# First expert rounds: most weight tiles planned behind the token gather, and all coarse flags on VectorE

## The chip, the cores and the metric

The kernel runs on one core of a Trainium2 chip. The metric is the device time in microseconds (us) of one execution; less is better. The engines are named as the profile does: PE is TensorE's matmuls and PEld its weight loads, DVE is VectorE, ACT is ScalarE, POOL is GpSimd, and SP is SyncE, which issues transfers.

## What is computed

```python
# attention: batch 8, heads 8, seq 576, head_dim 64; heads 0-3 a window of 32, heads 4-7 a dilated window (4 * 32)
scores = scale * np.matmul(q, k.transpose(0, 1, 3, 2))
scores = np.where(masks[None, :, :, :], scores, -1000000000.0)
attn = np.exp(scores - np.max(scores, axis=-1, keepdims=True))
attn = attn / (np.sum(attn, axis=-1, keepdims=True) + 1e-09)
x = np.matmul(attn, v)                    # -> (4608, 512)
# mixture of experts: N, D, E, F = 4608, 512, 8, 1024; cap = N // E
for idx in np.argsort(-(x @ w_gate).flatten()):
    tok, e = (int(idx) // E, int(idx) % E)
    if assigned[tok] >= 0 or counts[e] >= cap:
        continue
    assigned[tok] = e
    counts[e] += 1
for e in range(E):
    mask = assigned == e
    h = np.maximum(x[mask] @ w1[e], 0.0)
    out[mask] = h @ w2[e]
```

All tokens are ranked against all experts, and every expert takes exactly 576 tokens, each with its own best free choice in the order of the gate's values. Then each expert runs two matrix products on its tokens.

## The kernel before

The attention goes over 8 batches. Each makes scores (L485, L502, L505), exponentials (L455), the product with `v` (L513), the transposes of its result (L563) and the gate's logits (L596, L655). The result `xs` also goes to a scratch array `xd` in DRAM, a row for a token.

For each finished chunk of 128 tokens `coarse` makes a tile `pre` of flags (L756: is a constant table below the chunk's value), one instruction for a chunk, and PE counts them (`coarse_counts`, L761, two matmuls for a chunk). The last batch has five such chunks; there the first flag tile is made on POOL and the other four on DVE. When all are counted, L834 reads the sums on DVE, and the choice of the first expert begins.

The experts follow in 8 rounds. One round does this:

- A search finds the value at which an expert has its 576 tokens: eight steps, each with a compare on DVE (`G`, L781 or L783), nine count matmuls on PE (`pz`, L769) and a chain on DVE from `Q` (L806) to `F` (L816), with `base` (L794) and `kb` (L799) behind it. The steps of round r + 1 run while PE multiplies in round r.
- Behind the last step DVE chooses the expert (from `s`, L937, to `eidx`, L967). `fetch` brings its number to SP, which issues the loads of the weights: `weights("1", r, f, ...)` for eight tiles `raw` of 256 KB for `w1` and `weights("2", ...)` for eight of `w2` (L1141). The ring of `w1` holds 8 tiles, the ring of `w2` holds 4, so a round can issue twelve loads at once, and the last four of `w2` wait until the first four are converted.
- The listing turns the chosen tokens into `idx`: `ge` (L978), running sums on PE (L1015, L1016), `oa` and `ob` (L1061, L1074), sums on PE (`ptx`, L1081), `t` and `idx` (L1090 to L1093).
- POOL gathers the tokens from `xd` by `idx` in five transfers into `xg` (L1233). PE transposes them (`ptx`, L1246), ACT rounds to `xh` and DVE makes the rest `xl` (both by the helpers of L1128 and L1129).
- A weight is split in the same way: ACT makes `w1h`, `w2h` from `raw` and DVE makes `w1l`, `w2l` = `raw` - `w1h`, `w2h` (L1128, L1129).
- gemm1 (`ph`, L1283) is three matmuls for a pair of tiles (`xh w1h`, `xh w1l`, `xl w1h`), and `hb` its rectified result (L1128, L1303). gemm2 (`py`, L1325, and L1328 and L1330 for the last, half-filled group of tokens) gives `y`, which ACT writes; POOL scatters it to `out` (L1351).

No engine's order is written out. Each piece of work is given to a planner by `op(engine, cost, function, dependencies, boost)`. `run` walks over all pieces with these costs and dependencies, gives each a due time, moved by `boost`, and picks for each engine the next piece. It then writes the instructions in this order. Within an engine that order is fixed on the chip. What waits for what on the chip comes from the data of the tiles alone: a dependency that is given to the planner and has no data behind it decides places in an order, and is no wait. A transfer's time (`T_W` for a weight) is part of the planner's costs.

Of the kernel before, what the change touches and what calls it, by code (L numbers as in the profile page):

```python
# [38 lines left out]
B_L, B_G, B_T, B_X, B_H, B_HL, B_Y, B_S, B_W = 23000, 27000, 15000, 0, 15000, 11800, 28000, -15000, 1500  # L39
RAW1, D_R, NQ = 8, 262, (2, 2)  # L40
NS, B_E, DIRECT = (2, 2), 3000, 6
# [200 lines left out]
def attention(tc, ctx, C, load_const, T, xd, Lt, R):  # L242
# [388 lines left out]

    def coarse(c0, c1, x, late, other=0):
        for c in range(c0, c1):
            g, used, use_ = PRE.take()
            e = nc.gpsimd if c - c0 < other else nc.vector
            f = op("POOL" if c - c0 < other else "DVE", 600 if c - c0 < other else 290,
                   lambda c=c, g=g, e=e: R.coarse(c, g, e), [x, *used], late)
            counted[0] = op("PE", 60, lambda c=c, g=g: R.coarse_counts(c, g), [f, ready["c", 3], counted[0]], late)
            use_.append(counted[0])

    def tokens(un):
# [29 lines left out]
        x = un.op("DVE", 1000, lambda: R.choose(c0, c1), [*xs_, *(hl_ if b == B - 1 else ())], late)  # L671
        coarse(c0, c1, x, B_P if b < B - 1 else late - u * P_U, 0 if b < B - 1 else 1)

# [54 lines left out]
class Router:  # L728
# [24 lines left out]

    def coarse(self, c, g, eng):

        eng.tensor_scalar(g, self.C["coarse"], self.V0[:, c:c + 1], None, op0=OP.is_le)  # L756

# [340 lines left out]
def moe(tc, ctx, C, R, xd, w1, w2, out):  # L1098
# [30 lines left out]
    sub = lambda e, o, a, b: e.tensor_tensor(o, a, b, op=OP.subtract)  # L1129
    E, gemm1_end, x_users = {}, {}, {}  # L1130

# [94 lines left out]
    def gather(r, ix, box):  # L1226

        done = []
        for m, n in enumerate(MSZ):
# [5 lines left out]

            g = op("POOL", 1040, get, [ix, *old], B_G, lat=2100)
            if r == 0:
                pt, old, usep = (PYR if m % 3 < 2 else PTR).take()
            else:
                pt, old, usep = PTR.take()  # L1240
# [125 lines left out]
    def round_(r):  # L1366
        e = None
        if r:
            e = search(r) if r < NE - 1 else chain("DVE", 650, R.last, [st["fetch"], st["need"]])
        en = st["fetch"] = EN[r] = op("SP", 100, lambda: fetch(r, R.eidx), [e])  # L1370
        ix, BOX[r] = settle(r, e)
        X[r] = gather(r, ix, BOX[r])
        W[r] = [weights("1", r, f, [en]) for f in range(NF)]

    round_(0)
    for r in range(NE):
        W2 = [weights("2", r, f, [EN[r]]) for f in range(NF)]
        expert(r, X[r], BOX[r], W[r], W2)
# [80 lines left out]
```

## Time and profile before

| what | value |
|---|---|
| runs shown | 734.11, 725.01 and 735.1 us, median 734.11 |
| the profiled execution | 728.12 us |
| its span, first to last instruction | 726.4 us |
| PE busy | 680.5 us (94%) |
| DVE busy | 496.5 us (68%) |
| ACT busy | 279.9 us (39%) |
| POOL busy | 121.7 us (17%) |
| mean granted clock of PE | 0.958 |

Times inside the execution are us from the start of the span. The attention takes until about 210, the choice of the first expert and its listing until about 250, and the eight rounds the rest: round 0 multiplies from about 247 on, round 1 from about 309, round 2 from 357. A timeline row is one instruction, or several of one kind in a row (x4); in brackets stands the idle time of the engine before it and what ended it. The chain of waits is followed back from the last instruction, at each step to what released it.

### The profile page before, as it was taken

Reading aid. Unit: us, or ns where it says so; the run is one execution under the profiler, and the core shown is the slowest. Engines: PE = TensorE matmul, PEld = TensorE weight load, DVE = VectorE, ACT = ScalarE, POOL = GpSimd, SP = SyncE. Lnnn points to the kernel's source line nnn. Section 1 sums busy time; section 2 is a strip of 40 time slices with the busy share of each in tenths; the row PEclk is TensorE's granted clock in tenths of the full one; section 3 lists DMA queues with packets and bytes.
Section 4 is the critical chain, followed back from the end, with each engine's and each line's share of the span. In section 5 each row is a group of like instructions: output and inputs, shape, how many; then the busy total and the mean of one; then the engine's idle time right before and its main releaser. Section 6 shows DMA issues by size and latency. Waiting matters only on the chain.

```text
span 726.4 us, 17360 instructions
## 1 busy us (share of the span) xinstructions
PE 680.5 (94%) x6594; PEld 599.8 (83%) x6596; DVE 496.5 (68%) x2104; ACT 279.9 (39%) x593; POOL 121.7 (17%) x181
## 2 busy tenths in 40 slices
PE   8999999999974799898799999999999999999994
PEld 6888889999963698698579979978978978988983
DVE  5678877697248698788769969968977873733300
ACT  3455454453311531542423623523533534434210
POOL 6111111100000301400410410221131041031011
PEclk9999999999875799999899999999999999999998
DMA  9999999962112421711611712521441474132001
GB/s 255 264 263 293 286 288 268 271 170 67 34 34 87 153 59 44 254 52 51 219 55 49 247 44 66 190 109 52 140 159 51 147 238 155 43 95 95 1 22 44
DMA packets 55068, 98.32 MB, mean 135 GB/s; under 512 B 5828, under 2 KB 27460, under 8 KB 54980
## 3 DMA queue, kind: packets, MB, share of 16 engines
q1 hardware_dynamic: 49096, 78.32, 37.4%
q0 software_dynamic: 5888, 18.88, 7.8%
q8 instruction: 52, 0.85, 0.5%
q14 instruction: 32, 0.26, 0.1%
HBM read 78.31 MB, written 18.87 MB: 134 GB/s over the span
## 4 chain that ended last, share of the span: by engine, by line
PE 61%; DVE 13%; issue 12%; DMA 10%; POOL 2%; ACT 1%; SPq 0%; POOLq 0%; DVEq 0%
PE py L1325 15%; PE ph L1283 15%; PE pS L505 7%; PE px L513 5%; DMA xg<-xd,idx 3%; DMA qs<-in_qd 3%; PE px L563 2%; PE pS L502 2%; PE ptx L1246 2%; DVE hb L1303 2%; DMA k<-in_kd 2%; DVE G L783 2%; PE py L1328 2%; PE pm L485 2%; PE py L1330 2%
## 5 line engine op out<-in xcount | busy, mean ns | idle before, releaser
L1325 PE MATMUL py<-w2h,hb 128*128 128x512 f32 x512 | 172.6, 402 | 0.0
L1283 PE MATMUL ph<-xh,w1h 128*128 128x256 f32 (+1 forms) x512 | 139.1, 302 | 0.5 <-ACT xh L1128 0.5
L1283 PE MATMUL ph<-xh,w1l 128*128 128x256 f32 (+1 forms) x512 | 136.6, 297 | 0.0
L1283 PE MATMUL ph<-xl,w1h 128*128 128x256 f32 (+1 forms) x512 | 136.2, 297 | 0.0
L1325 PEld LDWEIGHTS py<-w2h,hb 128*128 128x128 f32 x512 | 97.1, 190 | 19.7
L1128 ACT ACTIVATE hb<-ph 128x256 fp32r<-128x256 f32 (+2 forms) x192 | 59.7, 346 | 116.8 <-PE ph L1283 116.7
L1325 PE MATMUL py<-w2l,hb 128*128 128x512 f32 x256 | 100.8, 394 | 1.0 <-DVE w2l L1129 1.0
L1283 PEld LDWEIGHTS ph<-xh,w1h 128*128 128x128 f32 x512 | 92.2, 190 | 1.2 <-ACT xh L1128 0.6
L1283 PEld LDWEIGHTS ph<-xh,w1l 128*128 128x128 f32 x512 | 91.9, 191 | 0.0
L1283 PEld LDWEIGHTS ph<-xl,w1h 128*128 128x128 f32 x512 | 91.5, 189 | 0.0
L505 PE MATMUL pS<-q,k 128*80 128x96 f32 (+1 forms) x672 | 84.4, 267 | 0.0
L1351 POOL DMA_INDIRECT out<-y,idx x40 | 41.0, 1025 | 227.3 <-ACT y L1128 159.4
L1303 DVE SCALAR_TENSOR_TENSOR hb<-ph,hb 128x256 fp32r<-128x256 f32 (+1 forms) x128 | 57.0, 451 | 25.7 <-ACT hb L1128 25.3
L455 ACT ACTIVATE E<-pS 96x384 f32<-96x384 f32 (+1 forms) x96 | 46.7, 486 | 70.9 <-PE pS L505 69.9
L505 PEld LDWEIGHTS pS<-q,k 128*80 128x80 f32 (+1 forms) x672 | 69.8, 161 | 0.0
L1128 ACT ACTIVATE y<-py 128x512 f32<-128x512 f32 (+1 forms) x40 | 23.9, 597 | 110.5 <-PE py L1325 98.5
L492 DVE CUSTOM_DVE_ANT_0 junkm<-pm,const 128x80 bf16<-128x80 f32 (+1 forms) x336 | 59.4, 243 | 6.6 <-PE pm L485 6.0
L1325 PEld LDWEIGHTS py<-w2l,hb 128*128 128x128 f32 x256 | 48.8, 190 | 10.2 <-DVE w2l L1129 1.5
L1129 DVE TENSOR_TENSOR w2l<-raw,w2h 128x512 fp32r<-128x512 f32 x64 | 42.1, 684 | 19.1 <-ACT w2h L1128 18.9
L1128 ACT ACTIVATE w1h<-raw 128x512 fp32r<-128x512 f32 x64 | 39.6, 629 | 35.9 <-DMA raw<-in_moe_w 35.5
L1233 POOL DMA_INDIRECT xg<-xd,idx x40 | 43.3, 1082 | 44.9 <-issue 25.1
L513 PE MATMUL px<-v,E 81*64 81x65 f32 (+1 forms) x1344 | 47.2, 224 | 0.8 <-ACT E L455 0.5
(165 smaller groups left out, 1009.7 us busy)
## 6 DMA issues: line engine op xcount, KB each, us to landing
raw<-in_moe_w SPq DMA_DIRECT2D x128, 256.0 KB, 4.4
v<-in_vp SPq DMA_DIRECT2D x8, 780.0 KB, 11.0
v<-in_vd SPq DMA_DIRECT2D x8, 650.0 KB, 11.3
xd<-xs SPq DMA_DIRECT2D x16, 288.0 KB, 8.8
xd<-xs SPq DMA_DIRECT2D x32, 144.0 KB, 10.7
qs<-in_qp SPq DMA_DIRECT2D x7, 576.0 KB, 11.0
k<-in_kp SPq DMA_DIRECT2D x7, 576.0 KB, 10.2
qs<-in_qd SPq DMA_DIRECT2D x7, 576.0 KB, 12.2
```

The source lines that it names most:

```text
L455: e = self.op("ACT", 380, lambda j=j, pS=pS: nc.scalar.activation(self.E[:self.nk, j * self.gs:j * self.gs + self.gs], pS.tile[:, :self.gs ...
L485: nc.tensor.matmul(pm[:, (c - c0) * self.nk:(c - c0 + 1) * self.nk], self.Qh[c], self.Kh[c], start=True, stop=True)
L492: nc.vector.tensor_tensor_reduce(out=jk[:, c - c0, :nk], in0=pm[:, (c - c0) * nk:(c - c0 + 1) * nk], in1=mm[:, min(1, (c if self.kind == 0 ...
L505: nc.tensor.matmul(pS[:nk, c - c0], self.Ks[c], self.Qm[c], start=False, stop=True, skip_group_check=True)
L513: nc.tensor.matmul(px[64 * a:64 * a + 64, c - c0], lh, self.V[c][a], start=True, stop=True)
L1128: act = lambda o, i, f=AF.Copy: nc.scalar.activation(o, i, f)
L1129: sub = lambda e, o, a, b: e.tensor_tensor(o, a, b, op=OP.subtract)
L1233: nc.gpsimd.indirect_dma_start(out=xg[:n], out_offset=None, in_=xd, in_offset=bass.IndirectOffsetOnAxis(ap=box[0][:n, m:m + 1], axis=0))
L1283: nc.tensor.matmul(o, a[:, d * 128:d * 128 + 128], b[:, d, c0:c1], start=((d, i) == pairs[0]), stop=((d, i) == pairs[-1]))
L1303: hl = op("DVE", 335 if j == 0 else 400, lambda: nc.vector.scalar_tensor_tensor(hb[:, CAP + c0:CAP + c1], o, 0.0, hb[:, c0:c1], op0=OP.max ...
L1325: nc.tensor.matmul(py, x, w, start=(f + i == 0), stop=(f == NF - 1 and i == 2))
L1351: s = nc.gpsimd.indirect_dma_start(out=out, out_offset=bass.IndirectOffsetOnAxis(ap=box[0][:n, m:m + 1], axis=0), in_=y[:n], in_offset=None)
```

## The change

The change has two parts.

First, a table `AHEAD_W=(3, 4)`: in round 0 the `w1` tiles from the fourth on, in round 1 those from the fifth on, and in both rounds all `w2` tiles, get the second gather of their round (`got[r, 1]`) as one more dependency, by `behind(r, f)`. Second, the last batch's first flag tile is made on DVE like the others; `coarse` loses the argument that chose the engine.

```diff
--- before.py
+++ after.py
@@ -37,7 +37,7 @@
 TOL_DVE, TOL_ACT, TOL_POOL, TOL_PE, T_W = 100, -50, 200, 500, 730
 T_P, T_S, AHEAD = 440, 2150, 5
 B_L, B_G, B_T, B_X, B_H, B_HL, B_Y, B_S, B_W = 23000, 27000, 15000, 0, 15000, 11800, 28000, -15000, 1500
-RAW1, D_R, NQ = 8, 262, (2, 2)
+RAW1, D_R, NQ, AHEAD_W = 8, 262, (2, 2), (3, 4)
 NS, B_E, DIRECT = (2, 2), 3000, 6
 B_C = (0, 0, 8000, 20000, 20000, 20000, 20000, 20000)
 P_U, B_A, B_K, B_V, B_P, TOL_A, TOL_B, TOL_C, TOL_D = 4680, 15400, -5200, 14500, -105500, 650, 650, 300, 800
@@ -629,12 +629,10 @@
         x = un.op("DVE", 800, lambda: R.choose(c0, c1), [x[0] for x in sm], B_K)
         coarse(c0, c1, x, B_P)
 
-    def coarse(c0, c1, x, late, other=0):
+    def coarse(c0, c1, x, late):
         for c in range(c0, c1):
             g, used, use_ = PRE.take()
-            e = nc.gpsimd if c - c0 < other else nc.vector
-            f = op("POOL" if c - c0 < other else "DVE", 600 if c - c0 < other else 290,
-                   lambda c=c, g=g, e=e: R.coarse(c, g, e), [x, *used], late)
+            f = op("DVE", 290, lambda c=c, g=g: R.coarse(c, g), [x, *used], late)
             counted[0] = op("PE", 60, lambda c=c, g=g: R.coarse_counts(c, g), [f, ready["c", 3], counted[0]], late)
             use_.append(counted[0])
 
@@ -669,7 +667,7 @@
         if b < B - 1:
             hl_.append(xs_[1])
         x = un.op("DVE", 1000, lambda: R.choose(c0, c1), [*xs_, *(hl_ if b == B - 1 else ())], late)
-        coarse(c0, c1, x, B_P if b < B - 1 else late - u * P_U, 0 if b < B - 1 else 1)
+        coarse(c0, c1, x, B_P if b < B - 1 else late - u * P_U)
 
     ch_, hl_ = {}, []
 
@@ -751,9 +749,9 @@
 
         self.pw = ctx.enter_context(self.tc.tile_pool(name="r_work", bufs=2))
 
-    def coarse(self, c, g, eng):
-
-        eng.tensor_scalar(g, self.C["coarse"], self.V0[:, c:c + 1], None, op0=OP.is_le)
+    def coarse(self, c, g):
+
+        self.tc.nc.vector.tensor_scalar(g, self.C["coarse"], self.V0[:, c:c + 1], None, op0=OP.is_le)
 
     def coarse_counts(self, c, g):
         nc = self.tc.nc
@@ -1127,7 +1125,7 @@
 
     act = lambda o, i, f=AF.Copy: nc.scalar.activation(o, i, f)
     sub = lambda e, o, a, b: e.tensor_tensor(o, a, b, op=OP.subtract)
-    E, gemm1_end, x_users = {}, {}, {}
+    E, gemm1_end, x_users, got = {}, {}, {}, {}
 
     def weights(n, r, f, deps):
 
@@ -1234,6 +1232,7 @@
                                              in_offset=bass.IndirectOffsetOnAxis(ap=box[0][:n, m:m + 1], axis=0))
 
             g = op("POOL", 1040, get, [ix, *old], B_G, lat=2100)
+            got[r, m] = g
             if r == 0:
                 pt, old, usep = (PYR if m % 3 < 2 else PTR).take()
             else:
@@ -1370,11 +1369,15 @@
         en = st["fetch"] = EN[r] = op("SP", 100, lambda: fetch(r, R.eidx), [e])
         ix, BOX[r] = settle(r, e)
         X[r] = gather(r, ix, BOX[r])
-        W[r] = [weights("1", r, f, [en]) for f in range(NF)]
+        W[r] = [weights("1", r, f, [en, *behind(r, f)]) for f in range(NF)]
+
+    def behind(r, f):
+
+        return [got[r, 1]] if r < len(AHEAD_W) and f >= AHEAD_W[r] else []
 
     round_(0)
     for r in range(NE):
-        W2 = [weights("2", r, f, [EN[r]]) for f in range(NF)]
+        W2 = [weights("2", r, f, [EN[r], *behind(r, NF)]) for f in range(NF)]
         expert(r, X[r], BOX[r], W[r], W2)
         if r + 1 < NE:
             round_(r + 1)
```

What this moves: the loads keep their order and their waits on SP. The rows are those of round 0's loads behind the fetch, before and after (`raw_3213` to `raw_3217` are tiles of the ring of `w1`; a row that waits would list it in brackets).

Before:

```order
L1141 ISA
L1141 DMA raw_3213<-in_moe_w 128x512
L1141 ISA
L1141 DMA raw_3214<-in_moe_w 128x512
L1141 ISA
L1141 DMA raw_3215<-in_moe_w 128x512
L1141 ISA
L1141 DMA raw_3216<-in_moe_w 128x512
L1141 ISA
L1141 DMA raw_3217<-in_moe_w 128x512
```

After:

```order
L1139 ISA
L1139 DMA raw_3213<-in_moe_w 128x512
L1139 ISA
L1139 DMA raw_3214<-in_moe_w 128x512
L1139 ISA
L1139 DMA raw_3215<-in_moe_w 128x512
L1139 ISA
L1139 DMA raw_3216<-in_moe_w 128x512
L1139 ISA
L1139 DMA raw_3217<-in_moe_w 128x512
```

Only line numbers differ. On DVE the places of the conversions move. The first place is the end of step 6 and the start of step 7 in the search that runs during round 0 (`kb` is the last of a step, `Q` the first behind the counts). Before:

```order
L816 TENSOR_SCALAR F_4138,delta<-F 128x32
L783 SCALAR_TENSOR_TENSOR G<-V_4033,delta,kb 128x36x16
L794 TENSOR_TENSOR base<-delta 128x1
L799 TENSOR_SCALAR kb<-const_65,base 128x17
L806 STREAM_TRANSPOSE Q<-pz 128x128
L808 TENSOR_REDUCE q<-Q 128x8
L811 TENSOR_SCALAR junk,flag<-q 128x8
L813 STREAM_TRANSPOSE F<-flag 128x32
L816 TENSOR_SCALAR F_4180,delta<-F 128x32
```

After:

```order
L814 TENSOR_SCALAR F_4133,delta<-F 128x32
L781 SCALAR_TENSOR_TENSOR G<-V_4026,delta,kb 128x36x16
L792 TENSOR_TENSOR base<-delta 128x1
L797 TENSOR_SCALAR kb<-const_65,base 128x17
L1127 TENSOR_TENSOR w2l_3252<-raw_3220,w2h_3236 128x512
L1127 TENSOR_TENSOR w2l_3253<-raw_3221,w2h_3237 128x512
L1127 TENSOR_TENSOR w2l_3254<-raw_3222,w2h_3238 128x512
L1127 TENSOR_TENSOR w2l_3255<-raw_3223,w2h_3239 128x512
L804 STREAM_TRANSPOSE Q<-pz 128x128
L806 TENSOR_REDUCE q<-Q 128x8
L809 TENSOR_SCALAR junk,flag<-q 128x8
L811 STREAM_TRANSPOSE F<-flag 128x32
```

The conversions of round 0's last four `w2` tiles (`w2l_3252` to `w2l_3255`) stand between `kb` and `Q` now; before, they stood earlier in the round, where those of the first four tiles stand now.

The second place is the last step of the search that runs during round 1, with the choice of the expert for round 2 behind it (`s` begins the choice). Before:

```order
L1303 SCALAR_TENSOR_TENSOR hb_3268<-ph_3205,hb_3268 128x256
L1303 SCALAR_TENSOR_TENSOR hb_3268<-ph_3207,hb_3268 128x320
L806 STREAM_TRANSPOSE Q<-pz 128x128
L808 TENSOR_REDUCE q<-Q 128x8
L811 TENSOR_SCALAR junk,flag<-q 128x8
L813 STREAM_TRANSPOSE F<-flag 128x32
L816 TENSOR_SCALAR F_4915,delta<-F 128x32
L819 TENSOR_SCALAR found<-delta,base 128x1
L1303 SCALAR_TENSOR_TENSOR hb_3269<-ph_3206,hb_3269 128x256
L937 TENSOR_SCALAR s<-const_65,delta 128x2
L938 TENSOR_TENSOR PR<-s,q 128x16
```

After:

```order
L1302 SCALAR_TENSOR_TENSOR hb_3268<-ph_3205,hb_3268 128x256
L1302 SCALAR_TENSOR_TENSOR hb_3268<-ph_3207,hb_3268 128x320
L1127 TENSOR_TENSOR w2l_3250<-raw_3222,w2h_3234 128x512
L804 STREAM_TRANSPOSE Q<-pz 128x128
L806 TENSOR_REDUCE q<-Q 128x8
L809 TENSOR_SCALAR junk,flag<-q 128x8
L811 STREAM_TRANSPOSE F<-flag 128x32
L814 TENSOR_SCALAR F_4913,delta<-F 128x32
L817 TENSOR_SCALAR found<-delta,base 128x1
L1302 SCALAR_TENSOR_TENSOR hb_3269<-ph_3206,hb_3269 128x256
L1127 TENSOR_TENSOR w2l_3251<-raw_3223,w2h_3235 128x512
L935 TENSOR_SCALAR s<-const_65,delta 128x2
```

Two conversions (`w2l_3250`, `w2l_3251`) came in, one directly ahead of `Q` and one directly ahead of `s`; before, they stood earlier in the round. From `PR` on DVE's order is the same in both kernels.

The third place is the start of round 1 on DVE, behind the compare `G` of the first step. Before:

```order
L1129 TENSOR_TENSOR w1l_3244<-raw_3216,w1h_3228 128x512
L1129 TENSOR_TENSOR xl<-ptx_3211,xh 128x4x128
L1129 TENSOR_TENSOR w1l_3245<-raw_3217,w1h_3229 128x512
L1129 TENSOR_TENSOR w1l_3246<-raw_3218,w1h_3230 128x512
L1129 TENSOR_TENSOR xl<-ptx_3211,xh 128x4x128
L1129 TENSOR_TENSOR w1l_3247<-raw_3219,w1h_3231 128x512
L1129 TENSOR_TENSOR w2l_3248<-raw_3220,w2h_3232 128x512
L1129 TENSOR_TENSOR xl<-ptx_3211,xh 128x4x128
L1345 TENSOR_TENSOR y_3273<-y_3273,py_3209 64x512
L1303 SCALAR_TENSOR_TENSOR hb_3271<-ph_3205,hb_3271 128x256
L1129 TENSOR_TENSOR w2l_3249<-raw_3221,w2h_3233 128x512
L1129 TENSOR_TENSOR xl<-ptx_3211,xh 128x4x128
```

After:

```order
L1127 TENSOR_TENSOR xl<-ptx_3211,xh 128x4x128 x2
L1127 TENSOR_TENSOR w1l_3244<-raw_3216,w1h_3228 128x512
L1344 TENSOR_TENSOR y_3273<-y_3273,py_3209 64x512
L1127 TENSOR_TENSOR xl<-ptx_3211,xh 128x4x128
L1302 SCALAR_TENSOR_TENSOR hb_3271<-ph_3205,hb_3271 128x256
L804 STREAM_TRANSPOSE Q<-pz 128x128
L806 TENSOR_REDUCE q<-Q 128x8
L809 TENSOR_SCALAR junk,flag<-q 128x8
L811 STREAM_TRANSPOSE F<-flag 128x32
L814 TENSOR_SCALAR F_4510,delta<-F 128x32
L781 SCALAR_TENSOR_TENSOR G<-V,delta,const_65 128x36x16
L797 TENSOR_SCALAR kb<-const_65,delta 128x16
```

Of the conversions `w1l` and `w2l` that stood among the `xl` only one `w1l` is left. On PE the counts of the first two steps there stand ahead of a transpose and of `xl` products that they stood behind; on ACT the conversions of the same weights stand behind the `xh` and the `y` of the rounds' starts.

## Rows read from the trace of the kernel before

**Rows 1.** Windows: us, busy us of each engine, granted clock, DMA share, GB/s.

```profile
150.00:200.00 50.00, 50.00 (x752) 46.73 (x751) 29.92 (x207) 19.88 (x41) 0.00 (x0) 0.93 0.31 75
...
376.00:434.00 58.00, 57.79 (x420) 50.68 (x419) 48.01 (x161) 23.41 (x52) 12.02 (x16) 1.00 0.34 114
```

**Rows 2.** Start, us, what: SP's timeline; chain of waits, gathers.

```profile
229.48 6.35 SPq L1141 DMA_DIRECT2D raw<-in_moe_w  x12
...
237.13 6.32 DMA xg<-xd,idx
...
298.66 3.84 DMA xg<-xd,idx
...
350.48 6.02 DMA xg<-xd,idx
```

**Rows 3.** Timeline: start us, us, engine, line, op, tiles, [idle before <-releaser]; last flags.

```profile
210.87 1.01 DVE L756 TENSOR_SCALAR pre<-const,V 128x256 bf16<-128x256 bf16 x4
211.05 1.09 POOL L756 TENSOR_SCALAR pre<-const,V 128x256 bf16<-128x256 bf16 x1 [74.06 <-DVE oh L880]
...
212.19 0.43 PE L761 MATMUL pz<-oh,pre 128*128 128x8 bf16 x10 [2.69 <-POOL pre L756]
212.74 0.17 DVE L834 TENSOR_SCALAR_CACHE_REDUCE junkc<-pz 128x8 f32<-128x8 f32 x1 [0.86 <-PE pz L761]
```

**Rows 4.** Timeline of DVE: round 0's search, steps 7 and 8; w2l.

```profile
280.75 0.32 DVE L806 STREAM_TRANSPOSE Q<-pz 128x128 f32<-128x128 f32 x1 [0.70 <-PE pz L769]
...
283.88 0.32 DVE L806 STREAM_TRANSPOSE Q<-pz 128x128 f32<-128x128 f32 x1 [0.93 <-PE pz L769]
...
349.74 2.49 DVE L1129 TENSOR_TENSOR w2l<-raw,w2h 128x512 fp32r<-128x512 f32 x4
```

**Rows 5.** Timeline and DMA queues (298.7 to 303): round 1's gather.

```profile
296.05 0.58 ACT L1128 ACTIVATE y<-py 128x512 f32<-128x512 f32 x1
...
296.42 0.33 DVE L1093 SCALAR_TENSOR_TENSOR idx<-t 64x5 int32<-64x5 f32 x2
...
296.90 1.46 POOL L1351 DMA_INDIRECT out<-y,idx  x1 [4.39 <-DVE idx L1093]
...
q1 hardware_dynamic: 113, 0.19, 11.9%
...
302.64 0.63 PE L1246 MATMUL ptx<-const,xg 128*128 128x128 f32 x4 [2.00 <-DMA xg<-xd,idx]
...
356.55 0.66 PE L1246 MATMUL ptx<-const,xg 128*128 128x128 f32 x4 [1.45 <-DMA xg<-xd,idx]
```

**Rows 6.** Chain of waits behind round 1's first ptx.

```profile
304.08 0.43 PE py L1328
...
307.60 0.23 PE py L1328
```

**Rows 7.** Timeline of DVE and PE: first search step of round 1.

```profile
313.04 0.30 DVE L806 STREAM_TRANSPOSE Q<-pz 128x128 f32<-128x128 f32 x1
...
314.10 0.85 PE L1283 MATMUL ph<-xh,w1h 128*128 128x320 f32 x4 [0.47 <-ACT xh L1128]
...
315.17 0.42 DVE L1129 TENSOR_TENSOR xl<-ptx,xh 128x256 fp32r<-128x256 f32 x1
```

**Rows 8.** Timeline: round 1's last search step, round 2's listing.

```profile
337.25 0.32 DVE L806 STREAM_TRANSPOSE Q<-pz 128x128 f32<-128x128 f32 x1
...
346.29 0.23 PE L1081 MATMUL ptx<-rx,ob 128*128 128x40 bf16 x3 [3.55 <-ACT w1h L1128]
```

**Rows 9.** Timeline of DVE at gather 0; chain of waits.

```profile
236.87 1.29 DVE L1129 TENSOR_TENSOR w1l<-raw,w1h 128x512 fp32r<-128x512 f32 x2
...
236.85 0.28 issue
...
349.54 0.16 DVE idx L1093
...
349.74 0.70 DVE w2l L1129
```

## Prediction

> **What bounds the kernel now.** I first read the busy time by stretches, to see where TensorE (PE) is the bound. In the attention it has no free time (50.00 of 50 us in 150 to 200), and from 376 on each expert round of about 57.8 us is filled by it (57.79 of 58.00) [rows 1]. So an edit can pay or cost only between 200 and 376: in the last selection, in the listing of round 0, in round 1, and in the listing of round 2. What is won or lost there is carried to the end unchanged, since behind it PE runs without a gap; the orders of PE, ACT and DVE from the end of round 1's search on are those of before.
>
> Then the chain of waits. In this stretch it goes three times through the gather of the tokens: 6.32, 3.84 and 6.02 us from its start to its landing [rows 2]. The weight loads of a round share the 16 DMA engines with it: the twelve of round 0 are issued from 229.48 on, for 6.35 us, just ahead of its gather [rows 2]. That is what the change's few words name. Last I read VectorE (DVE) around the search, since its row of subtractions (`w1l`, `w2l`, 0.62 to 0.74 us each) is what the order moves.
>
> **The loads: nothing moves on the chip.** The twelve loads of round 0 are in the same order on SP before and after, and none of the loads behind the first carries a wait. The added dependency lives only in the planner: it makes the tile of a load no later on the chip than it was, since no data goes from the gather to the load. So the 6.32 us of gather 0 stay, 0 us; were the wait real, the gather could land as fast as 3.84, a gain of 2.48 (a rival below). What does move is the place that the planner gives to everything that hangs on those loads: the conversions on ACT and DVE, and by them steps of the search.
>
> **Flags, -0.35.** Before, four flag tiles take DVE 1.01 from 210.87 (0.25 each), the fifth takes POOL 1.09 from 211.05, to 212.14; PE's ten count matmuls start at 212.19 and DVE's L834 follows at 212.74 [rows 3]. After, the fifth ends on DVE at 210.87 + 1.01 + 0.25 = 212.13, no sooner; but eight of ten matmuls (0.43 us in all) have run beside it, and two are left, 0.09. That gives 212.13 + 0.05 + 0.09 + 0.12 (the gap that L834 had behind the matmuls' end) = 212.39, so 0.35 sooner. All engines are in this chain, so it carries. Bounds: 0, if the matmuls still wait for one semaphore, and -0.5.
>
> **Round 0's search.** Four `w2l` now stand between `kb` and `Q` of step 7. Before, `Q` began at 280.75 after 0.70 idle, so DVE was free from 280.05; four `w2l` in a row take 2.49 [rows 4]. So `Q` begins at 280.05 + 2.49 = 282.54, 1.79 later. Step 8 had 0.93 idle ahead of its `Q` [rows 4], of which I count 0.6 as absorbed, because its counts now stand ahead of six `w2` matmuls on PE that they stood behind. Left: +1.17 for the choice of the expert, `idx` and the loads of round 1. PE itself has other work there and loses some 0.5 on the first of the four `w2l`. Cover gone, the whole 1.79 shows.
>
> **Round 1's gather.** The delay meets a gain. The first gather stands on POOL behind the scatter of 296.90, which waits for a `y` that ACT writes at 296.05, behind conversions of `w1h` [rows 5]; two of these now stand behind `y`, and the scatter can start near 296.0, so the gather is held by `idx` (two `idx` of 0.33 from 296.42 on [rows 5], so 296.75 + 1.17 = 297.9) and goes at 298.2, against 298.66. The loads, 1.17 later, run into it: before, 0.19 MB of them were left behind 298.7 [rows 5], at that window's peak rate about 0.5 us; now 0.5 + 1.17 + 0.45 = 2.1 us. The gather lands at 298.2 + 3.84 = 302.0 if it isn't held by them, at 302.0 + 1.7 = 303.7 if it waits out what is added; I take the middle, 302.9, against 302.64 for PE's first `ptx` before. PE gets there later too, at 301.65 (0.5 from round 0, 0.2 by the later listing, and one pair of matmuls, 0.46, that stands ahead of `ptx` now), so it waits 1.25.
>
> Here the clock decides. Before, PE waited 2.00 and then ran at 1.2 GHz: a `py` matmul took 0.43 at 304.08, and 0.23 at 307.60 [rows 6]. Eight matmuls at 0.2 more is 1.6 us. In round 2 a wait of 1.45 [rows 5] left the clock at 2.4 GHz. With 1.25 I take the clock as kept: -1.6.
>
> **Round 1's start.** Step 1 of the search, 2.13 us of DVE from `Q` at 313.04 to 315.17, now stands ahead of an `xl` that it stood behind, and step 2 ahead of the next [rows 7]. PE waits for these `xl`: of two steps, 4.26, it covers some 1.75 with three groups of four products that need no `xl` (about 0.6 each, the distance from 314.10 to the next group), and about 2.5 is left, an estimate. Of it 0.47 is idle that PE has anyway, at 314.10 [rows 7], and 0.38 is work that stands behind the fourth counts now, not ahead. To the fourth counts of the search: +0.26 (gather) - 1.6 (clock) - 0.46 (the pair done early) + 2.5 - 0.85 = **-0.15**. With the gather at 302.0 it is -0.7; with it at 303.7, a wait of 2.05 and the clock at 1.2 GHz, +1.4 to +2.2.
>
> **Round 2's listing, +1.2.** Two more `w2l` come late in round 1's search: one directly ahead of `Q` of step 8 (337.25 [rows 8]), one between the last `hb` and `s`. Each costs DVE 0.60 apart. Behind them stand, in one chain, the choice of the expert, `ge`, PE's running sums, `ob`, and the `ptx` sums for which PE already waits 3.55 at 346.29 [rows 8]. There is nothing to hide 1.2 us, and gather 2, at 350.48, goes as much later. Bounds: +0.6 if one of them falls into time in which DVE waits anyway, +1.4 if each takes the 0.70 that a single one has between its neighbours [rows 9].
>
> **Where a rule bears on it.** Gather 0 started 0.28 after `idx` while DVE ran `w1l`; gather 2 starts only when a `w2l` of 0.70 has ended, 0.78 after `idx` [rows 2, 9]. The trace shows both, and my 298.2 takes the first. The Trainium skill (SBUF — State Buffer, section "SBUF: two separate sides") says that a transfer issued from GpSimd stalls while VectorE holds the port that the two share, since its descriptors can't be written. By it the sum would be some 0.45 more; gather 2 would agree, gather 0 does not.
>
> **Sum.** -0.35 - 0.15 + 1.2 = +0.7. The profiled execution took 728.12 (its span is 726.4), so 728.8. The three runs shown of the kernel lie from 725.01 to 735.1 with a median of 734.11, 6 us over the profiled one; I add half of that, +3, since the median of after can come from either end: **731.8**.
>
> **Rivals.**
> A, the forecast: +0.7 (-0.2 to +1.8).
> B, gather 1 comes late and PE falls to 1.2 GHz: -0.35 + 2.2 + 1.2 = +3.05, so 731.2 on the profiled basis, 734.2 as above. For it: twelve loads made gather 0 6.32; against: the loads are nearly done by then.
> C, the attention's other order keeps the clock up. Some rows of attention move with the due times, and PE's clock is 0.93 in 150 to 200 [rows 1], 0.07 x 50 = 3.5 us of it; if three quarters come back, -2.6, so -1.9 in all, 726.2 (729.2 as above). Nothing in the moved rows says that they should.
> D, the other side: slower by over 2%. The half clock of round 1, if PE's wait grows past the 2.00 of before, would have to last 29 us, where each us at 1.2 GHz loses half: 14.6 us. Before it lasted from 302.64 to about 307 [rows 6]. It decides from a gather that lands after 303.7.
> E, the loads do wait: gather 0 lands up to 2.48 sooner, -1.8 in all, 726.3 (729.3 as above). Against it: the unchanged rows of SP.
>
> **Chances.** A 0.63, B 0.20, C 0.10, D 0.04, E 0.03. About 2% (14.6 us) is what a measurement of this kernel can tell from no change. A, B, C and E are all within it, whichever run is taken: same 0.94, slower 0.04 (D), and faster 0.02, taken from C, in case the attention gains far more than that. The range runs from 724.0 (C or E against the fastest run, 725.01 - 1) to 738.5 (B against the slowest, 735.1 + 3.05); A's own range is 727.9 to 733.6.
>
> **What would show it.** Right: SP issues twelve loads in one go at the start of round 0; L834 about 0.35 after its place; four `w2l` between `kb` and `Q` near 280 and a `Q` about 1.8 later; the first `ptx` of round 1 after a wait under 1.5 and `py` matmuls of 0.23 behind it; PE idle on `xl` near 312; `idx` of round 2 some 1.2 later than the counts. Wrong: a gap in SP's loads; gather 0 landing in 4 us; `py` of 0.43 behind the first `ptx`; other than 57.8 us for a later round, which I hold fixed.

## The result

| | before | after |
|---|---|---|
| median of 20 runs | 731.84 us | 735.34 us |
| lowest to highest | 723.15 to 736.9 | 729.03 to 741.27 |
| the profiled execution | 728.12 (span 726.4) | 735.71 (span 733.7) |
| mean granted clock of PE | 0.958 | 0.953 |

The ratio is 1.0064, with a 95% interval of 1.0038 to 1.0089: the change makes the kernel 4.7 us slower (2.8 to 6.5), two thirds of a per cent. The ratio goes by fast runs alone (17 of the 20 before, 19 after), so it is not that of the medians of all runs, which lie 3.5 apart. The forecast was +0.7 us. The number 731.8 is 3.5 under the median of after, inside the range of 724.0 to 738.5, but it stood below the median of 734.11 then shown, and the time moved the other way.

The page of after and two of its windows (columns as in [rows 1]) differ little from before: PE is full in the attention and in the later rounds.

```profile
span 733.7 us, 17362 instructions
...
PE 683.8 (93%) x6596; PEld 600.4 (82%) x6596; DVE 497.0 (68%) x2105; ACT 278.2 (38%) x593; POOL 120.2 (16%) x180
```

```profile
150.00:200.00 50.00, 49.97 (x757) 46.46 (x756) 33.12 (x225) 20.83 (x42) 0.00 (x0) 0.94 0.36 96
...
382.00:440.00 58.00, 57.62 (x417) 50.55 (x416) 48.12 (x161) 23.41 (x52) 12.03 (x16) 1.00 0.34 114
```

The 7.3 us between the two spans are not all the change's. Up to about 54 us the orders of all engines are the same in both kernels, and at VectorE's 251st instruction, at 55.13 in before, after is already 3.3 us late (58.45). The chain of waits goes through the transfers of the first batches there, and the `k` transfer in it starts at 47.59 in after and at 43.97 in before. The fourteen traces of this case, of equal orders up to that instruction, reach it between 54.54 and 61.02. So single spans say little here, and the comparison goes by stage, over several traces.

Stage by stage the steps of the prediction can be found in the trace of after; what became of the clock is told further below. SP issues the twelve loads of round 0 in one go, in 6.46 us as against 6.35 (timeline of SP, as [rows 2]):

```profile
235.15 6.46 SPq L1139 DMA_DIRECT2D raw<-in_moe_w  x12
```

The flags (timeline, as [rows 3]):

```profile
216.94 1.07 DVE L754 TENSOR_SCALAR pre<-const,V 128x256 bf16<-128x256 bf16 x5
...
217.28 1.00 PE L759 MATMUL pz<-oh,pre 128*128 128x8 bf16 x10 [1.72 <-DVE pre L754]
218.41 0.17 DVE L832 TENSOR_SCALAR_CACHE_REDUCE junkc<-pz 128x8 f32<-128x8 f32 x1 [0.40 <-PE pz L759]
```

From the start of the flags to L834 (L832 in the changed file) it is 1.47 us now, 1.87 before, so 0.40 sooner; forecast 0.35. The four `w2l` at step 7 of round 0's search (timeline of VectorE, as [rows 4]):

```profile
283.72 0.24 DVE L797 TENSOR_SCALAR kb<-const,base 128x17 f32<-128x17 f32 x1
283.86 2.49 DVE L1127 TENSOR_TENSOR w2l<-raw,w2h 128x512 fp32r<-128x512 f32 x4
286.27 0.31 DVE L804 STREAM_TRANSPOSE Q<-pz 128x128 f32<-128x128 f32 x1
...
289.11 0.32 DVE L804 STREAM_TRANSPOSE Q<-pz 128x128 f32<-128x128 f32 x1 [0.61 <-PE pz L767]
```

`Q` waits for nothing now but the `w2l` ahead of it, and step 8 keeps 0.61 of its 0.93 idle. The gathers of rounds 0 to 2 (chain of waits, as [rows 2]) follow; gather 0's 5.35 can't be put down to the gate, since with the orders of before it took 5.47 to 6.32 in six traces, and 5.51 to 6.43 in the three others with the gate's orders (6.05 in the gate alone):

```profile
242.80 5.35 DMA xg<-xd,idx
...
303.26 3.93 DMA xg<-xd,idx
...
356.04 6.42 DMA xg<-xd,idx
```

And the end of round 1's search with the listing behind it (timeline of VectorE and PE, as [rows 8]):

```profile
341.60 0.68 DVE L1127 TENSOR_TENSOR w2l<-raw,w2h 128x512 fp32r<-128x512 f32 x1
342.20 0.31 DVE L804 STREAM_TRANSPOSE Q<-pz 128x128 f32<-128x128 f32 x1
...
343.93 0.68 DVE L1127 TENSOR_TENSOR w2l<-raw,w2h 128x512 fp32r<-128x512 f32 x1
344.53 0.22 DVE L935 TENSOR_SCALAR s<-const,delta 128x2 f32<-128x2 f32 x1
...
351.85 0.26 PE L1079 MATMUL ptx<-rx,ob 128*128 128x40 bf16 x3 [3.56 <-ACT w1h L1126]
```

Both `w2l` stand without idle time between their neighbours, so each holds the chain up by its 0.60, and PE waits 3.56 ahead of the sums behind them, 3.55 before.

### The profile page after: what moved, and what is told of

Its sections match the earlier page's. It is cut to its first block, busy times and chain, and to the rows that moved or that the text cites. A ratio compares the mean times of both kernels' runs of the same rounds, so it can differ in the third digit from the quotient of the medians.

```text
span 733.7 us, 17362 instructions
## 1 busy us (share of the span) xinstructions
PE 683.8 (93%) x6596; PEld 600.4 (82%) x6596; DVE 497.0 (68%) x2105; ACT 278.2 (38%) x593; POOL 120.2 (16%) x180
## 4 chain that ended last, share of the span: by engine, by line
PE 54%; DVE 16%; issue 14%; DMA 9%; POOL 3%; ACT 1%; SPq 1%; POOLq 0%; DVEq 0%
PE py L1324 13%; PE ph L1282 10%; PE pS L505 8%; PE px L513 6%; DMA xg<-xd,idx 5%; DVE hb L1302 3%; PE px L563 2%; PE pS L502 2%; DVE G L781 2%; PE pm L485 2%; PE ptx L1245 2%; DMA k<-in_kd 2%; PE px L653 2%; PE py L1327 2%; PE py L1329 1%
## 5 line engine op out<-in xcount | busy, mean ns | idle before, releaser
L492 DVE CUSTOM_DVE_ANT_0 junkm<-pm,const 128x80 bf16<-128x80 f32 (+1 forms) x336 | 59.4, 243 | 5.4 <-PE pm L485 5.0
L513 PEld LDWEIGHTS px<-v,E 81*64 81x64 f32 (+1 forms) x1344 | 43.0, 138 | 9.7 <-issue 2.8
## 6 DMA issues: line engine op xcount, KB each, us to landing
k<-in_kp SPq DMA_DIRECT2D x7, 576.0 KB, 10.2
```

The lines of the kernel that those rows point to most:

```text
L492: nc.vector.tensor_tensor_reduce(out=jk[:, c - c0, :nk], in0=pm[:, (c - c0) * nk:(c - c0 + 1) * nk], in1=mm[:, min(1, (c if self.kind == 0 ...
L513: nc.tensor.matmul(px[64 * a:64 * a + 64, c - c0], lh, self.V[c][a], start=True, stop=True)
```

## The experiments

A ratio is against the kernel before on the same chip. At first three explanations stood against each other: the moved rows of the attention cost (theory A), the expert rounds cost (B), or nothing in one place does (C). The attention and the expert rounds are planned by two separate planners, so the flags part moves only the attention, and the gate only the rounds; each can be run alone.

**The flags part alone** (measured twice, on different occasions): the last batch's call of `coarse` no longer asks for POOL, which does what the diff's lines on `coarse` do, and nothing of `AHEAD_W` is there.

> The flags part alone; the gate is left out, so every engine's order from round 0 on is that of the kernel before, and the orders in the attention are those of the changed kernel. The change as a whole measured +4.7 us (ratio 1.0064). Theory A (the attention's moved rows cost it): the ratio is 1.005 to 1.008, +4 to +6, with the flags' own step still about 0.35 to 0.4 sooner between the start of the last flags and L834. Theory B (the expert rounds cost it): 0.9995, -0.35, within 0.998 to 1.002. Theory C (nothing in one place; the attention's transfers fall out differently in each execution): 0.998 to 1.003, and the start of the last flags stands between 208 and 217 without order.

> The flags part alone once more, as a second trace. Theory P: from the last product with v to L834 10.3 to 11.3 us again (9.3 to 9.8 in the kernels with the attention's old order), since the half clock begins under 3.3 us behind that product; ratio 1.001 to 1.004. If it takes 9.8 or less, the moved rows of the attention do not cost and the three earlier traces were chance.

Measured: 1.0005 (0.9973 to 1.0036) and 1.0005 (0.997 to 1.004).

**The gate alone**: all of `AHEAD_W`, `got` and `behind`, and `coarse` as before.

> The gate alone; the last batch's first flag tile stays on GpSimd, and the orders up to the end of the attention are those of the kernel before. Theory A (attention): ratio 0.999 to 1.002 (the traces give -1.07 from gather 0 to gather 1 and +0.96 from gather 1 to gather 2). Theory B (rounds): 1.005 to 1.008, with gather 2 at least 2 us later, counted from L834, than in the kernel before, or later rounds over 57.8 us. In both: four w2l in a row between kb and Q of step 7, and a first ptx of round 1 with less than 2 us of wait and matmuls of 0.23 behind it.

Measured: 1.0018 (0.9991 to 1.0045). That is below the 1.005 to 1.008 that theory B asked for, and inside theory A's 0.999 to 1.002, although the trace has the steps that were expected in it (table below).

**The two halves of the flags part.** One kernel has the changed plan without the changed instruction, the other the changed instruction in the old plan:

```diff
 # e3_plan, against before
-e = nc.gpsimd if c - c0 < other else nc.vector
-f = op("POOL" if c - c0 < other else "DVE", 600 if c - c0 < other else 290,
+e = nc.gpsimd if other and c - c0 < 1 else nc.vector
+f = op("DVE", 290,
 # e4_vector, against before (planned as POOL, 600)
-e = nc.gpsimd if c - c0 < other else nc.vector
+e = nc.vector
```

> No gate, and the first of the last batch's flag tiles runs on GpSimd as before, but the planner counts it as a piece of VectorE (290): so the attention has the changed kernel's orders without the changed instruction. Theory A (the moved rows): 1.005 to 1.008, about 0.4 us slower than the flags part alone. Theory B: 1.000 within 0.002. If instead the instruction on VectorE is what costs (it holds up other work there), this kernel is at 1.000 and the flags part alone is above.

Measured: 1.0035 (1.0004 to 1.0065).

> No gate, and the planner counts the first of the last batch's flag tiles as a piece of GpSimd (600) as before, but it runs on VectorE: so every order is that of the kernel before but for this one instruction. Theory A and theory B both: -0.35 to -0.4 from the start of the last flags to L834, ratio 0.9995, which a measurement will not tell from 1.000. If it is over 1.003, the instruction itself costs, not the places of others.

Measured: 0.9973 (0.9942 to 1.0003).

Theory A is not borne out: the plan without the instruction came out slower, but between what theory A (1.005 to 1.008) and theory B (1.000 within 0.002) asked for, and the whole flags part, twice, did not. In the traces the last product with `v` to L834 took 8.8 to 11.3 us in the five executions with the moved rows and 9.4 to 10.6 in the nine without; the first three pointed to the order (10.3 to 11.3), and the repeats (10.1 and 8.8) took that away. What the stretch takes follows the moment at which PE's clock falls to 1.2 GHz, 2.6 to 5.0 us behind that product with either order.

**The gate in one round only**: `AHEAD_W` is (3,) or (9, 4) instead of (3, 4).

> The gate in round 0 only (AHEAD_W = (3,)), no flags part. The four w2l between kb and Q of step 7 are there, and none of round 1's w2l stands in the last step of its search. So far two gated traces took 68.5 us from the last w2l of round 0's gemm1 (256 in the kernel before) to the end of the fourth step of round 1's search (325), counted without what the half clock cost, and three ungated ones 66.3. Theory A (the cost comes from round 0's delayed search): +1.3 between steps 7 and 8 as in both gated traces, about 67.6 or more for that stretch, and 17.17 from the fourth step to ge, as before. Theory B (it comes from round 1's gated places): 66.3 + 1.3, of which the wait for the loads takes back some, so under 67.0. Ratio 1.000 to 1.003.

Measured: 1.0009 (0.9975 to 1.0044).

> The gate in round 1 only (from the fifth w1 tile on, and all of w2), no flags part. Round 0's search is that of the kernel before: no +1.3. w2l stand ahead of Q of step 8 and ahead of s as in the change. Theory A (round 0's delayed search): 66.3 for the stretch from 256 to 325, without the half clock, and +1.2 from the fourth step to ge (18.35 against 17.17). Theory B (round 1's places, where search steps stand ahead of xl): 67.0 or more, and the same +1.2. Ratio 1.001 to 1.003.

Measured: 1.003 (1.0001 to 1.006).

The ratios don't separate the two, but the traces (table below) separate the places. The stalls at the start of round 1 come with the gate in round 0: between PE's first `ptx` and the fourth `Q` of the search PE is idle for 1.83 us in e5_round0 and for 0.57 in e6_round1, as with the old orders. The late `w2l` come with the gate in round 1: from the 4th to the 8th `Q` and on to `PR` e6_round1 takes 1.55 and 0.85 more than before, e5_round0 nothing more.

**The gate on `w1` only.**

```diff
-W2 = [weights("2", r, f, [EN[r], *behind(r, NF)]) for f in range(NF)]
+W2 = [weights("2", r, f, [EN[r]]) for f in range(NF)]
```

> The gate on the w1 tiles alone (w2 is not gated), no flags part. The four w2l between kb and Q of round 0's step 7 are not in this order (one stands there), and round 1's two late w2l are. If the four w2l are what delays round 1: steps 7 and 8 cost +0.3 or less instead of +1.3, the stretch from 256 to 325 takes 66.3 to 67.3 (without the half clock), and the +1.2 or more to ge stays. Ratio 1.000 to 1.003.

Measured: 0.9991 (0.9958 to 1.0023). One `w2l` stands at step 7 and costs nothing (timeline of VectorE): it lies in the idle time that [rows 4] show there, and 0.1 of that is left. So the delay of round 0's search comes from the four `w2l`, that is from the gate on `w2`. The late `w2l` of round 1 stay, at 1.56 and 0.85.

```profile
283.28 0.24 DVE L799 TENSOR_SCALAR kb<-const,base 128x17 f32<-128x17 f32 x1
283.43 0.69 DVE L1129 TENSOR_TENSOR w2l<-raw,w2h 128x512 fp32r<-128x512 f32 x1
284.22 0.32 DVE L806 STREAM_TRANSPOSE Q<-pz 128x128 f32<-128x128 f32 x1
...
287.35 0.32 DVE L806 STREAM_TRANSPOSE Q<-pz 128x128 f32<-128x128 f32 x1 [0.93 <-PE pz L769]
```

**The change again, and the change without the attention's moved rows** (the gate, and the flag of e4_vector).

> The change once more, as a second trace and beside its parts on one chip. Theory P (the parts add up): attention's order +1.1 to +1.5 in the last 10 us of the attention (from the last product with v to L834 10.3 to 11 us, against 9.3 to 9.8), +1.3 at steps 7 and 8 of round 0's search, +1.17 from the fourth step of round 1's search to ge, PE's first ptx of round 1 with no or little half clock behind it, ratio 1.005 to 1.007. Theory N (the 1.0064 was the draw of the executions): 1.002 or less.

Measured: 1.006 (1.0026 to 1.0094).

> The gate, and the first of the last batch's flag tiles on VectorE, but counted by the planner as a piece of GpSimd, so that the attention keeps the orders of the kernel before: the change without the moved rows of the attention. Theory P (the parts add up): 1.5 us less than the change, ratio 1.002 to 1.005. If the moved rows of the attention cost nothing: the same ratio as the change. If they are all of it: 0.999 to 1.001.

Measured: 1.0043 (1.0007 to 1.0079). So the slowdown comes again, and it is there without the moved rows of the attention too: this points to the rounds and the gate (theory B). How much of it is the gate's the runs leave open. With the flag's instruction the gate costs 0.5 to 5.8 us, and the gate alone (e2_gate) is not told from no change; neither it nor the flags part alone reaches the change's ratio. Whether the moved rows cost something beside the gate was not settled.

**Where the gate costs.** This table has, for each trace, the time in us from one start to the next, read from VectorE's and PE's timelines: from the 6th to the 8th `Q` of round 0's search; from the first `ptx` (of the gathered tokens) of round 1 to the 4th `Q` of its search; from there to the 8th; from the 8th `Q` to the first `Q` of the next search; and, over all, from L834 to the end.

| kernel | Q6 to Q8 | ptx to Q4 | Q4 to Q8 | Q8 to next Q1 | L834 to the end |
|---|---|---|---|---|---|
| before | 6.26 | 20.61 | 13.99 | 32.61 | 513.62 |
| e1_flags | 6.26 | 19.40 | 14.00 | 32.71 | 509.87 |
| e12_flags | 6.26 | 19.04 | 14.01 | 32.79 | 510.83 |
| e3_plan | 6.26 | 19.04 | 13.99 | 34.39 | 514.31 |
| e4_vector | 6.26 | 19.04 | 13.99 | 33.21 | 512.24 |
| e8_wait_only | 6.26 | 19.04 | 13.99 | 32.13 | 511.31 |
| after | 7.57 | 20.31 | 14.56 | 33.81 | 515.31 |
| e9_change | 7.62 | 22.55 | 14.56 | 35.11 | 519.11 |
| e2_gate | 7.58 | 20.46 | 14.56 | 34.72 | 516.32 |
| e10_gate_flag | 7.62 | 20.40 | 14.56 | 32.99 | 515.70 |
| e5_round0 | 7.57 | 21.61 | 13.99 | 31.60 | 512.91 |
| e6_round1 | 6.27 | 19.21 | 15.54 | 32.33 | 513.77 |
| e11_w1_only | 6.26 | 19.92 | 15.55 | 32.09 | 511.26 |
| e7_wait | 7.58 | 22.79 | 14.56 | 32.55 | 517.54 |

The first six have the orders of before in the rounds, the next four those of the change. By the means of the two groups the rounds take 512.0 and 516.6 us, 4.6 more. The traces of each group scatter by some 1.7 us (standard deviation), so the 4.6 is good to about 2.6 either way. It is near the 4.4 to 4.7 that the runs of the whole change measure, but two of its four traces are of the gate without the moved rows, for which the runs measure 1.3 and 3.1. The second column is the one to look at: five of six traces of the old orders have 19.04 to 19.40, and the kernel before, on whose trace the prediction was made, 20.61.

The reason is PE's clock. These are the first `ptx` of round 1 and a `py` behind it (timeline of PE) in the flag kernel with the old orders (e4_vector), in the flags part (e12_flags, the same orders in the rounds), and in after:

```profile
301.54 0.63 PE L1246 MATMUL ptx<-const,xg 128*128 128x128 f32 x4 [1.32 <-DVE w1l L1129]
...
302.92 0.39 PE L1328 MATMUL py<-w2h,hb 128*128 128x512 f32 x1
```

```profile
305.72 0.63 PE L1246 MATMUL ptx<-const,xg 128*128 128x128 f32 x4 [1.86 <-DMA xg<-xd,idx]
...
307.12 0.40 PE L1328 MATMUL py<-w2h,hb 128*128 128x512 f32 x1
```

```profile
307.33 0.63 PE L1245 MATMUL ptx<-const,xg 128*128 128x128 f32 x4 [1.65 <-DMA xg<-xd,idx]
...
308.73 0.40 PE L1327 MATMUL py<-w2h,hb 128*128 128x512 f32 x1
```

In each the `py` is at the pace of 2.4 GHz (0.39 or 0.40 as the timeline counts it, 0.23 from one to the next), behind a wait of 1.32, 1.86 and 1.65. In the kernel before it ran at 1.2 GHz behind a wait of 2.00 [rows 5, 6]; the timeline counts such a `py` as 0.63. The windows of 3.30 us behind `ptx` have the granted clock in the third column from the end: 0.50 in before, 1.00 in e4_vector.

```profile
303.88 0.63 PE L1328 MATMUL py<-w2h,hb 128*128 128x512 f32 x1
...
303.30:306.60 3.30, 3.30 (x9) 2.04 (x8) 1.89 (x3) 2.14 (x3) 2.44 (x5) 0.50 0.56 180
```

```profile
302.20:305.50 3.30, 3.30 (x18) 2.36 (x17) 2.28 (x4) 3.15 (x6) 2.44 (x5) 1.00 0.47 150
```

With the same orders the clock fell there in one trace of six; in the five others PE had waited 1.18 to 1.86. The length of the wait alone does not decide it, for in e5_round0 PE waited longer than in before and kept its clock:

```profile
301.25 0.63 PE L1247 MATMUL ptx<-const,xg 128*128 128x128 f32 x4 [2.10 <-DMA xg<-xd,idx]
...
302.00:305.30 3.30, 3.30 (x18) 2.40 (x17) 2.35 (x4) 3.18 (x5) 1.99 (x4) 1.00 0.61 194
```

So the change does not keep a clock that was lost before; mostly it was not lost.

What the gate adds at that place is stalls, as the prediction said. PE's waits between that `ptx` and the 4th `Q` in after, with the window from the one to the other, and the same in e4_vector:

```profile
316.47 0.45 PE L767 MATMUL pz<-G,ohr 128*128 128x64 bf16 x9 [0.77 <-DVE G L781]
317.21 0.46 PE L1245 MATMUL ptx<-const,xg 64*128 64x64 f32 x4 [0.29 <-DVE xl L1127]
318.14 0.85 PE L1282 MATMUL ph<-xh,w1h 128*128 128x320 f32 x4 [0.47 <-ACT xh L1126]
...
320.21 0.85 PE L1282 MATMUL ph<-xl,w1h 128*128 128x320 f32 x4 [0.22 <-DVE xl L1127]
...
307.33:327.64 20.31, 18.55 (x154) 16.80 (x155) 15.17 (x45) 11.27 (x24) 3.71 (x6) 1.00 0.18 55
```

```profile
311.43 0.85 PE L1283 MATMUL ph<-xh,w1h 128*128 128x320 f32 x4 [0.47 <-ACT xh L1128]
...
301.54:320.58 19.04, 18.46 (x154) 16.70 (x155) 15.80 (x46) 11.39 (x24) 4.01 (x6) 1.00 0.31 96
```

By the windows PE is idle for 1.76 us of 20.31 and for 0.58 of 19.04 (a wait of 0.10 is too short to be listed): 1.18 more. Its busy time is 18.55 against 18.46. Together that is the difference of the column (20.31 to 20.46 in three traces of the change's orders against 19.04).

These stalls may cost a clock of their own, which the prediction did not count. In e9_change PE ran at 1.2 GHz from 314.31 to 317.72 behind them, and likewise for 3.41 us in e5_round0 and e7_wait; in the three other kernels with `w2` gated in round 0 it did not, and in none of the eight without that gate was there a half clock at this place. From e9_change:

```profile
314.40:317.70 3.30, 3.30 (x20) 3.10 (x20) 2.81 (x13) 0.55 (x2) 0.00 (x0) 0.50 0.00 0
```

**Loads that really wait.** Since the gate lives only in the planner, two kernels were to make it true: behind the second gather, GpSimd writes one element of the tile of the first gated load. The first has the gate's plan too, the second the old plan.

```diff
+                if m == 1 and r < len(AHEAD_W):
+                    nc.gpsimd.memset(RAW["1"].tiles[AHEAD_W[r]][:1, :1], 0.0)
```

> The gate alone as before, with the same orders on every engine, and the loads now really wait: behind the second gather GpSimd writes one element of the tile of the first gated load, and SP's loads behind it stand in line. The planner's picture is now true on the chip. If the gate's idea is right (the loads slow the gather down): gather 0 lands about 4 us after its start instead of 6.3, the first products of round 0 start 1.5 to 2.5 sooner than in the gate alone, and the ratio falls from 1.002 to 0.999. If the loads cost the gather nothing: it stays, and the weights come later: idle time of PE on w1h or w1l of the fourth tile, ratio 1.003 or more.

Measured: 1.0103 (1.0058 to 1.0148, six runs), 6 us slower than the gate alone. SP's twelve loads now take 15.33 us (timeline of SP):

```profile
234.00 15.33 SPq L1141 DMA_DIRECT2D raw<-in_moe_w  x12
```

The five groups of `ptx` and `py` transposes of round 0 (timeline of PE), first with the wait (gather 0 started at 241.66), then in the gate alone (238.18):

```profile
245.57 0.87 PE L1249 MATMUL py<-const,xg 128*128 128x128 f32 x4 [1.92 <-DMA xg<-xd,idx]
247.90 1.11 PE L1249 MATMUL py<-const,xg 128*128 128x128 f32 x4 [1.03 <-DMA xg<-xd,idx]
249.76 1.09 PE L1249 MATMUL ptx<-const,xg 128*128 128x128 f32 x4 [0.32 <-DMA xg<-xd,idx]
...
252.85 0.63 PE L1249 MATMUL py<-const,xg 128*128 128x128 f32 x4 [0.30 <-DMA xg<-xd,idx]
...
254.91 0.46 PE L1249 MATMUL py<-const,xg 64*128 64x64 f32 x4 [0.95 <-DMA xg<-xd,idx]
```

```profile
244.27 1.12 PE L1247 MATMUL py<-const,xg 128*128 128x128 f32 x4 [3.82 <-DMA xg<-xd,idx]
245.61 1.06 PE L1247 MATMUL py<-const,xg 128*128 128x128 f32 x4
...
250.63 0.46 PE L1247 MATMUL py<-const,xg 64*128 64x64 f32 x4
```

The first tokens come 3.9 us behind the gather's start instead of 6.1: the loads do slow the gather down. But the last come after 13.2 us instead of 12.5, since the held loads now run beside gathers 1 to 4, and each of those is waited for. In round 1 the stretch to the 4th `Q` grows to 22.79, with 0.93 of waiting for the gather and the 3.41 us of half clock in it. So what rival E supposed of a real wait came half true: the first tokens come sooner, but the collision moves to the later gathers, and the kernel is slower. From L834 to the end the two traces differ by only 1.2 us (517.54 and 516.32), so what makes up the rest of the 6 us is not shown.

> All orders of the kernel before, the first of the last batch's flag tiles on VectorE, and the real wait of the loads behind the second gather in rounds 0 and 1 by one written element, without the gate in the planner. The flag alone measured 0.997. Theory: if the loads slow the gather, 1.5 to 2.5 us sooner at the first products of round 0, ratio 0.994 to 0.996; if ACT and DVE, whose orders here expect the weights early, stand still on a conversion of the fourth tile ahead of xh or xl, PE waits for that instead and the ratio is 1.000 or more.

Measured: 1.0005 (0.9973 to 1.0037), and a miss: with the old plan the load stands ahead of the gather in the program, so the written element came behind the load. SP issued its loads in one go and nothing waited; the element was written at 242.51, behind ACT's reading of that tile (238.11) and ahead of VectorE's (242.63), so what is left is a zero in one element of a `w1` tile in each of the two rounds. In time the kernel is a second look at e4_vector; the two together, 0.9973 and 1.0005, do not tell the flag's 0.4 us from nothing.

## Why the prediction was wrong

- **What bounds the kernel**: right. Only the stretch between the selection and round 2 moved; later rounds follow the old orders, and from search to search they take 57.7 to 59.0 us with the old orders and 57.8 to 59.7 with the change's.
- **The loads, nothing moves on the chip**: right. SP issued its twelve loads in one go.
- **Flags, -0.35**: measured 0.40 from the flags to L834. Right in the sum: the five tiles took 1.07, not 1.26, and L834 followed 0.40 behind them, not 0.26.
- **Round 0's search, +1.17**: 1.31 to 1.36 from the 6th to the 8th `Q`, in every trace with `w2` gated in round 0, and 0 in every other. Right but for 0.15, and two misses met in it: `Q` of step 7 came 1.60 later, not 1.79, and step 8 gave back 0.3, not 0.6. (1.79 less 0.6 is 1.19, not 1.17.)
- **Round 1's gather, PE's first `ptx` +0.26**: against the first `Q` of round 0's search, PE's first `ptx` stood at 43.16 in before and at 43.63 to 43.93 in the four traces of the change's orders. 0.2 to 0.5 more than forecast. The six traces of the old orders lie from 42.66 to 43.67, so by the means it is 0.7 later. The wait was 1.65 in after and 1.28 to 1.51 in the three others, for 1.25 (its terms, 300.64 + 0.5 + 0.2 + 0.46, give PE at 301.80, not 301.65, and so a wait of 1.10).
- **The clock, -1.6**: this is the step that failed. Its size was right, since before took 20.61 there and most others of its orders 19.04. But the half clock of [rows 6] belonged to one execution, not to the kernel; five other traces of the same orders do not have it, and in e5_round0 even a wait of 2.10 left the clock full. The change cannot give back what is mostly not lost. Without this term the forecast for the stretch is +1.45 instead of -0.15, and the sum +2.3. That is 1.6 of the 4.0 us between forecast and result; the rest is in the points below.
- **Round 1's start**: stalls of 2.5, less 0.85, less the pair done early of 0.46, so 1.19 behind `ptx`: measured 1.27 to 1.42 in three traces. That the net fits is in good part luck: PE's idle time grew by 1.18 where 2.03 (2.5 less the 0.47 idle before) was forecast, and the 0.84 of work that was to leave the stretch did not show, for PE's busy time grew by 0.09. The fourth trace, e9_change, has 22.55, with the half clock that its stalls brought. (With the gather at 302.0 the same sum gives -1.05, not the -0.7 given.)
- **Round 2's listing, +1.2**: 0.56 from the 4th to the 8th `Q`, and 0.60 from there to `PR`: 1.16. Right in size. From the 8th `Q` to the next search's first the traces of the change have 34.16 on average and the others 32.97, so 1.2 where 0.6 was due. The rest goes with the clock, since in the listing there are 10.2 to 13.7 us at 1.2 GHz with the change's orders and 6.8 to 13.7 without; but single traces of either group scatter by 2 us there, so that it is the change's is not shown.
- **The rule weighed**: I took the 0.28 behind `idx` of gather 0, and the rule was nearer. In all nine traces in which the scatter was out of the way in time, the four of the change's orders among them, the first gather of round 1 started 0.78 behind `idx` and 0.05 behind the end of a `w1l` (after: rows below). That is 0.5 later than I had it, and about the 0.2 to 0.5 by which `ptx` was late. It is near the 0.45 that the prediction took from the Trainium skill's rule (SBUF — State Buffer, section "SBUF: two separate sides"); what that passage tells is that a VectorE operation in a two-port mode keeps GpSimd from writing the descriptors, and that the subtraction `w1l` does so is a reading that no run here shows. Whether the shared port held the gather, or the place of the `w1l` in VectorE's order, was not tried; gather 0 starts 0.29 behind `idx` in all fourteen traces.

```profile
302.15 0.33 DVE L1091 SCALAR_TENSOR_TENSOR idx<-t 64x5 int32<-64x5 f32 x2
302.52 0.69 DVE L1127 TENSOR_TENSOR w1l<-raw,w1h 128x512 fp32r<-128x512 f32 x1
...
303.26 0.97 POOL L1231 DMA_INDIRECT xg<-xd,idx  x1 [1.78 <-issue]
```

- **The sum**: without the clock's credit -0.35 + 1.45 + 1.2 = +2.3, of which 2.65 in the rounds; the traces show 4.6 in the rounds, the runs 4.7 over all. Of the 1.95 between, by the means of the traces, 0.45 is the later `ptx` of round 1, 0.4 the stretch behind it (mostly the half clock that one of the four traces has there, 3.41 us of it), 0.55 round 2's listing, and about 0.7 lies behind the first `Q` of the search in round 2, where orders are the same and single traces differ by 1 us and more (356.6 against 357.3 to the end, on average); 0.15 goes the other way, ahead of round 0's search. The last two are not the change's as far as the traces tell.
- **Rival B** (slower by 3.05) had the place right and not the cause: `ptx` came 0.2 to 0.5 later than forecast, not 0.8 or more, and behind it the clock stayed full in all four traces of the change's orders. **Rival C** fell (the attention did not gain); the flags part alone at 1.0005 twice leaves its moved rows a cost of some 0.8 us, with 1.7 either way, so this stays open, and what the plan of e3_plan did to come out at 1.0035 too. **D**: no half clock of such a length in round 1, where the longest was 3.41 us. **E**: SP's loads did not wait, as the prediction held against it; what a real wait does is told above.
- **The number 731.8** has 3 us added to the profiled execution, half of the way to the median shown, so a forecast of slower by 0.7 came out under the 734.11 of the kernel itself. That after's median lies in the range says little, since the range spans the scatter of the runs. (Its upper end, 735.1 + 3.05, is 738.15, not 738.5.)

## What to carry to other kernels

Before a clock loss in the one trace at hand is counted as something that a change gives back, look whether it is there in other executions of the same order: here PE lost its clock behind a wait of 2.00 us in one trace and kept it behind 0.51 to 2.10 in thirteen. A dependency that only a planner sees moves no transfer; it moves the work of other engines behind it, here conversions onto the search's chain, and there each one costs its full 0.6 us where no idle time of that size is left. And a planner that is told the truth about a wait is not thereby right: the kernel with the true wait was slower (1.0103) than the one with the false (1.0018).

## What was not expected of the hardware

With equal orders of PE, ACT and VectorE, the stretch from L834 to the end took 509.9 to 514.3 us in six executions, and the time to VectorE's 251st instruction 54.5 to 61.0 us in fourteen. In the last stretch of the attention the stretch of 1.2 GHz ahead of the last product with `v` was 6.8 us long in seven traces, 3.4 in five, and missing in two, and the time from one maximum on VectorE (L492, at 178.12 in before) to that product followed it: 24.9 to 25.0 us with 6.8, 23.4 to 23.5 with 3.4, and 21.8 without.
